# Native W_out products in column halves, from blocks that lie in natural order

## The chip, the cores and the metric

The kernel runs on one core of a Trainium2 chip. The metric is the device time of one execution in microseconds (us). A run of the kernel before comes with the median of three executions, and one more execution was taken by the hardware profiler; the trace below is of that one.

## What is computed

Attention with a sliding window of 128 and 4 sink positions, over 4 batches, 8 heads, 768 positions and head size 64, and behind it a two-layer perceptron with a leaky rectifier, all in fp32:

```python
def _moe_ref(x, w_in, w_out, alpha):           # x: 3072 x 512, the attention's output
    h = x @ w_in                               # 512 x 2048
    g = np.maximum(h, 0.0) + alpha * np.minimum(h, 0.0)
    return (g @ w_out).astype(np.float32)      # 2048 x 512
```

## The kernel before

The 3072 tokens are worked in 12 chunks (c) of 256. The 2048 inner columns are 16 blocks (f) of 128, each with its part of w_in and of w_out (W_out below). For every chunk and block, `gemm1` makes a 128 x 256 tile of h in PSUM (L991), ScalarE and VectorE make g of it (L995, L996), and `gemm2` adds g times the block of W_out to two banks of 128 tokens x 512 columns, one for each half j of the chunk.

Most products are made in three fp32r steps: g and the weights are split in a high and a low part, and high x high, high x low and low x high are added (L1048, L1049, L1046, the last for the low part of g). The weights arrive as 64-bit floats and are converted on the chip in the first 150 us (`convert_weights`). For the first WHOLE = 8 blocks and the first two chunks, W_out is not split yet: `convert_weights` leaves it whole in a tile `entire` (L440), g isn't split either, and one native fp32 product a half stands in for the three steps (`whole` in `gemm2`, L1037). In the trace such a product has two passes, so two records for each half. The two chunks and eight blocks make 16 such products of two halves, 64 records. Later, for chunk 2, `divide` splits these eight blocks (L476 the cast to the high part, on ScalarE or VectorE, L479 the subtraction).

A W_out block lies with its 256 even columns ahead of its 256 odd ones, since the host writes it so; whoever reads it goes across both halves (`"p (y x) -> p x y"`), so that neighbouring columns come from places 256 elements apart, and the result has the natural order.

The attention's values (`values`, L873; L971 for the last chunks) are native too, with 64 stationary columns each: two heads write to partitions 0 to 63 and 64 to 127 of one bank, in the two column halves of the array. Scores of the first two chunks (L670) are native products of two halves of 64 rows.

Nothing of the order on the engines is written out. Every operation is an `op` with an engine, an estimated cost, what it reads and writes, and `Plan.draw` simulates the engines with these costs and takes, for each engine, the ready operation of the lowest rank; `Plan.issue` writes the instructions in that order. For TensorE an operation may have a mode; where two operations that follow each other differ in it, the draw adds 0.16 us if one of the two is "col" and else 0.1. In the first 60 us, TensorE is given filling matmuls (L1221) where the draw sees it idle.

Of the kernel before, what the change touches and what calls it, by code (L numbers as in the profile page):

```python
# [9 lines left out]
F32 = mybir.dt.float32  # L10
# [7 lines left out]
ALU = mybir.AluOpType  # L18

P = 128  # L20
B, H, S, D = 4, 8, 768, 64
DM, DF = 512, 2048
# [6 lines left out]
NF = DF // P  # L29
# [28 lines left out]
WHOLE = 8  # L58
# [28 lines left out]
class Plan:  # L87
# [20 lines left out]
    def held(self, tile_):  # L108
        v = Value(None)
        v.at = tile_  # L110
        return v
# [197 lines left out]
def dve(n, fast=False):  # L309
    return 0.07 + (0.52e-3 if fast else 1.04e-3) * n  # L310


def cast(n, psum=False):
    return (0.045 if psum else 0.092) + 0.84e-3 * n
# [22 lines left out]
def woven(n):  # L337
    return 0.003 + 0.4167e-3 * n


def native(n):
    return 1.667e-3 * n
# [3 lines left out]
ISSUE = 0.45  # L346
SINKLAG = 0.0
R_TAIL, N_TAIL, T_TAIL = 0.2, 0.65, 0.36


def program(ctx, tc, qk, pairs, vp, vq, vs, w, par, out):
    nc = tc.nc
# [5 lines left out]
    op, val, held = plan.op, plan.value, plan.held  # L358
# [36 lines left out]
    raws, fins = {}, {}  # L395
# [7 lines left out]


    def home(f):
        return f + NF - WHOLE if f < WHOLE else f

    def load_weights(f, engine="ACT"):
        raw = raws[f] = held(None)

        def run():
            raw.at = const.tile([P, 2 * DM, 2], I32, tag=f"w{home(f)}", name="wraw")
            (nc.sync if engine == "SP" else nc.scalar).dma_start(
                raw.at.rearrange("p (i x) w -> p i (x w)", i=2), w[f].bitcast(I32).rearrange("i p x -> p i x"))
        return op(engine, ISSUE if engine == "SP" else 0.12, run, writes=[raw] + (lent.get(home(f), []) if f < WHOLE else [raws[f - NF + WHOLE]]), nbytes=8 * P * 2 * DM)

    def convert_weights(f):
        raw, fin, wa = raws[f], Block(None), val("wa")
# [51 lines left out]

    def divide(f):
        fin, entire = fins[f], entires[f]

        def high(engine):
            fin.at[1] = const.tile([P, 2, DM], F32R, tag=f"out{f - 1}", name="wout")
            (nc.scalar.copy if engine == "ACT" else nc.vector.tensor_copy)(fin.at[1][:, 0], entire.at)  # L476
        op("ACT", cast(DM), lambda: high("ACT"), reads=[entire], writes=[(fin, 2)] + ([entires[f - 1]] if f else []),
           other=("DVE", dve(DM, True), lambda: high("DVE")))
        op("DVE", dve(DM), lambda: nc.vector.tensor_tensor(  # L479
            fin.at[1][:, 1], entire.at, fin.at[1][:, 0].bitcast(F32), ALU.subtract), reads=[entire, (fin, 2)], writes=[(fin, 3)])  # L480

    stage, vtile, vst = {}, {}, {}

    lent = {}
# [64 lines left out]
    part, alt = param[:, :4], param[:, 4:].bitcast(F32)  # L549
# [313 lines left out]
    turned = {}  # L863
# [143 lines left out]
    def gemm2(c, f, dst):  # L1007
        gh, gl = gs.pop((c, f))
        fin = fins[f]
        begin, end = (WHOLE % NF, (WHOLE - 1) % NF) if c == 2 else (0, NF - 1)  # L1010
        if f == begin:
            acc[c] = [val("pa"), val("s")] if c == 1 else [val("o"), val("o")]
        o2 = acc[c]
        if c == NCHUNK - 1 and f >= NF - 2:
            latest.append((f, fin, gh, gl))
            for j in range(2 if f == NF - 1 else 0):
                for x, fin, gh, gl in latest:
                    def last(j=j, x=x, fin=fin, gh=gh, gl=gl):
                        js = slice(j * P, (j + 1) * P)
                        nc.tensor.matmul(o2[j].at, gh.at[:, js], fin.row(0), start=False, stop=False)  # L1020
                        nc.tensor.matmul(o2[j].at, gh.at[:, js], fin.row(1), start=False, stop=False)
                        nc.tensor.matmul(o2[j].at, gl.at[:, js], fin.row(0), start=False, stop=x == NF - 1)
                    op("PE", 3 * woven(DM), last, reads=[fin, gh, gl], writes=[o2[j]], tail=R_TAIL)
                ob = val("ob")
                for n, cols in enumerate((slice(0, DM // 2), slice(DM // 2, DM)) if j else (slice(0, DM),)):
                    op("ACT", cast(cols.stop - cols.start, True), lambda ob=ob, j=j, cols=cols: nc.scalar.copy(ob.at[:, cols], o2[j].at[:, cols]),  # L1026
                       reads=[o2[j]], writes=[(ob, n)])
                    by, cost, engine = ("ACT", 0.1, nc.scalar) if n == j else ("SP", ISSUE, nc.sync)
                    op(by, cost, lambda ob=ob, j=j, cols=cols, engine=engine: engine.dma_start(dst(j)[:, :, cols], ob.at[:, cols]),
                       reads=[(ob, n)], nbytes=4 * P * (cols.stop - cols.start))  # L1030
            return
        if c < 2 and f < WHOLE:
            entire = entires[f]

            def whole():
                for j in range(2):
                    nc.tensor.matmul(o2[j].at, gh.at[:, j * P:(j + 1) * P], entire.at.rearrange("p (y x) -> p x y", y=2),  # L1037
                                     start=f == begin, stop=False)
            op("PE", 2 * native(DM), whole, reads=[entire, gh], writes=o2, tail=N_TAIL)
            return  # L1040
        for lowpart in range(2):
            def some(lowpart=lowpart):
                for j in range(2):
                    js = slice(j * P, (j + 1) * P)
                    if lowpart:
                        nc.tensor.matmul(o2[j].at, gl.at[:, js], fin.row(0), start=False, stop=(f == end))  # L1046
                    else:
                        nc.tensor.matmul(o2[j].at, gh.at[:, js], fin.row(0), start=(f == begin), stop=False)  # L1048
                        nc.tensor.matmul(o2[j].at, gh.at[:, js], fin.row(1), start=False, stop=False)  # L1049
            op("PE", (2 if lowpart else 4) * woven(DM), some, reads=[fin, gl if lowpart else gh], writes=o2, tail=R_TAIL)  # L1050
        if f == end:
            for j in range(2):
                ob = val("ob")
                op("ACT", cast(DM, True), lambda ob=ob, j=j: nc.scalar.copy(ob.at, o2[j].at), reads=[o2[j]], writes=[ob],
           other=("DVE", dve(DM), lambda ob=ob, j=j: nc.vector.tensor_copy(ob.at, o2[j].at)) if 0 < c < 3 else None)
                op("SP", ISSUE, lambda ob=ob, j=j: nc.sync.dma_start(dst(j), ob.at), reads=[ob], nbytes=4 * P * DM)
            del acc[c]
# [109 lines left out]
    def dst(c):  # L1167
        return lambda j: out[c * QC:(c + 1) * QC].rearrange("(y j x) d -> j x y d", y=2, j=2)[j]
# [9 lines left out]
    n = 0  # L1178
# [35 lines left out]
    for a in pend:  # L1214
        gemm2(*a, dst(a[0]))
# [27 lines left out]
    gen = ctx.enter_context(tc.tile_pool(name="general", bufs=1))  # L1243
# [3 lines left out]
    wts = [fins[f].at for f in range(NF)]  # L1247
    with tc.If(bad != 0, label="general"):
        for f in range(NF):
            for i in range(2):  # L1250
                general_weights(nc, gen, w[f, i], wts[f][i])
        with tc.For_i(0, B, 1) as b:
            for cc in range(CPB):
                x = general(nc, gen, ptile, cc, b, qk5, vp5, nsink, window, ident)
                acc = [ptile("o", 2) for _ in range(2)]
                for f in range(NF):
                    general_moe(nc, gen, ptile, f, x, wts[f], alt, acc)
                for j in range(2):
                    ob = gen.tile([P, DM], F32, tag="ob", name="ob", bufs=3)
                    nc.scalar.copy(ob, acc[j])  # L1260
                    nc.gpsimd.dma_start(out5[b, cc, j], ob)
# [24 lines left out]
        nc.tensor.matmul(acc[j], gl[:, js], rows[0], start=False, stop=(f == NF - 1))  # L1286


def general_weights(nc, gen, src, dst):
    raw = gen.tile([P, DM, 2], I32, tag="wraw", name="wraw", bufs=2)  # L1290
    nc.gpsimd.dma_start(raw.rearrange("p x w -> p (x w)"), src.bitcast(I32))
    a = gen.tile([P, DM], I32, tag="wa", name="wa", bufs=2)
    low, high, af = raw[:, :, 0], raw[:, :, 1], a.bitcast(F32)
    nc.scalar.activation(af, high.bitcast(F32), AF.Abs)
    nc.vector.tensor_scalar(af, af, EXP_LOW, EXP_HIGH, op0=ALU.max, op1=ALU.min)
    nc.vector.tensor_scalar(a, a, 3, 0x3FFFFFFF, op0=ALU.logical_shift_left, op1=ALU.bitwise_and)
    nc.vector.scalar_tensor_tensor(a, high, -0x40000000, a, op0=ALU.bitwise_and, op1=ALU.bitwise_or)
    nc.scalar.activation(low, low.bitcast(U32), AF.Copy, scale=2.0 ** -29)
    nc.vector.tensor_tensor(a, a, low, ALU.add)
    nc.scalar.copy(dst[:, 0], af)  # L1300
    nc.vector.tensor_tensor(dst[:, 1], af, dst[:, 0].bitcast(F32), ALU.subtract)


def general(nc, gen, ptile, cc, b, qk5, vp5, nsink, window, ident):
# [118 lines left out]
```

## Time and profile before

| | us |
|---|---|
| median of three executions | 652.11 (651.16 to 652.94) |
| the profiled execution | 651.43 |
| its span, first to last instruction | 649.9 |
| busy in the span: TensorE | 640.4 (99%) |
| VectorE | 522.6 (80%) |
| ScalarE | 392.4 (60%) |

PE is TensorE's matmuls, PEld its loads of stationary operands, DVE VectorE, ACT ScalarE, POOL GpSimd. Matmuls are pipelined: a record lasts from its start to the arrival of its last result, and the next may start long before. So what an instruction costs is read from start to start, not from its duration, and a busy TensorE is not one without waits. Where a native matmul is followed by an fp32r one, the record of the latter starts early and lasts longer; the start of the one after it tells when the native one was through. An operand shape such as 128*64 128x512 is 128 rows by 64 stationary columns, then the moving operand.

### The profile page before, as it was taken

How to read it: one execution, taken by the hardware profiler on the slowest of the kernel's cores; microseconds unless marked ns; L12 is line 12 of the kernel's file. 1: busy time of each engine (PE TensorE's matmuls, PEld its weight loads, DVE VectorE, ACT ScalarE, POOL GpSimd, SP SyncE). 2: the span in 40 equal slices, each digit the busy share in tenths (PEclk: the TensorE clock that was granted, in tenths of full speed). 3: DMA queues.
4: the chain of work that ended last, by engine and by line, in shares of the span. 5: the costliest groups of instructions: out<-in, count | busy, mean ns of one | idle time of the engine just before them, and what ended most of it. 6: DMA issues, size and time to landing. Idle time of an engine off the chain costs nothing. (4 is left out here: it accounts for less than half of the span.)

```text
span 649.9 us, 13096 instructions
## 1 busy us (share of the span) xinstructions
PE 640.4 (99%) x4495; PEld 563.0 (87%) x4497; DVE 522.6 (80%) x1748; ACT 392.4 (60%) x1060; POOL 34.1 (5%) x115
## 2 busy tenths in 40 slices
PE   8999999989999999999999999999999999999997
PEld 3666667979998999999999999998999998998996
DVE  6998888997987987895996997895996997895332
ACT  6997677856646646645645754844754854752332
POOL 2120000000100000000100000000100000000000
PEclk9999999999999999999999999999999999999999
DMA  8776631333443444341633534432534424421001
GB/s 314 250 274 219 215 101 53 96 99 106 129 135 120 136 138 135 112 131 50 188 120 91 168 98 138 136 112 82 169 113 115 148 97 147 148 65 51 33 3 35
DMA packets 58825, 82.29 MB, mean 127 GB/s; under 512 B 9088, under 2 KB 35328, under 8 KB 58752
## 3 DMA queue, kind: packets, MB, share of 16 engines
q1 hardware_dynamic: 55200, 68.41, 33.3%
q10 hardware_dynamic: 3552, 12.98, 5.7%
q8 instruction: 37, 0.61, 0.4%
q14 instruction: 36, 0.29, 0.1%
HBM read 64.33 MB, written 17.04 MB: 125 GB/s over the span
## 5 line engine op out<-in xcount | busy, mean ns | idle before, releaser
L995 ACT ACTIVATE g<-bank,param 128x256 f32<-128x256 f32 x192 | 90.9, 473 | 94.4 <-PE bank L991 93.8
L991 PE MATMUL bank<-xh,win 128*128 128x256 f32 x768 | 140.5, 279 | 0.0
L991 PE MATMUL bank<-xh,w 128*128 128x256 f32 x768 | 139.1, 276 | 0.4 <-DVE g L996 0.4
L991 PEld LDWEIGHTS bank<-xh,w 128*128 128x128 f32 x768 | 120.9, 192 | 2.7 <-DVE g L996 1.0
L991 PEld LDWEIGHTS bank<-xh,win 128*128 128x128 f32 x768 | 120.8, 192 | 2.3 <-issue 1.6
L1001 ACT CAST gh<-g 128x256 fp32r<-128x256 f32 x176 | 70.6, 405 | 63.0 <-DVE g L996 62.4
L996 DVE TENSOR_TENSOR g<-bank,g 128x256 f32<-128x256 f32 x192 | 80.1, 420 | 33.8 <-ACT g L995 32.4
L991 PE MATMUL bank<-xl,win 128*128 128x256 f32 x384 | 105.7, 275 | 0.0
L991 PE MATMUL bank<-xl,w 128*128 128x256 f32 x384 | 105.6, 275 | 0.0
L700 ACT ACTIVATE pt<-pt,nm 128x260 f32<-128x260 f32 (+1 forms) x192 | 93.5, 489 | 16.5 <-DVE nm L694 16.2
L694 DVE CUSTOM_DVE_ANT_0 pt<-bank,masks 128x260 f32<-128x260 f32 (+1 forms) x192 | 71.2, 401 | 33.0 <-PE bank L680 29.3
L1002 DVE TENSOR_TENSOR gl<-g,gh 128x256 fp32r<-128x256 f32 x176 | 73.4, 421 | 17.6 <-ACT gh L1001 14.5
L991 PEld LDWEIGHTS bank<-xl,win 128*128 128x128 f32 x384 | 73.6, 192 | 2.3 <-issue 1.4
L991 PEld LDWEIGHTS bank<-xl,w 128*128 128x128 f32 x384 | 73.5, 192 | 1.2 <-issue 0.4
L1048 PE MATMUL bank<-w,gh 128*128 128x512 f32 x188 | 71.6, 381 | 0.0
L1049 PE MATMUL bank<-w,gh 128*128 128x512 f32 x188 | 71.2, 379 | 0.0
L641 ACT CAST kq<-stage 128x392 fp32r<-128x392 f32 (+1 forms) x80 | 39.1, 488 | 36.8 <-PE bank L680 28.2
L1048 PE MATMUL bank<-wout,gh 128*128 128x512 f32 x160 | 60.7, 379 | 0.0
L1049 PE MATMUL bank<-wout,gh 128*128 128x512 f32 x160 | 60.6, 379 | 0.0
L1046 PE MATMUL bank<-w,gl 128*128 128x512 f32 x188 | 56.4, 382 | 0.0
L1046 PE MATMUL bank<-wout,gl 128*128 128x512 f32 x160 | 47.7, 380 | 0.0
L745 POOL TENSOR_TENSOR sink<-pt,ri 128x8 f32<-128x8 f32 x80 | 20.2, 254 | 502.0 <-DVE ri L730 421.9
(150 smaller groups left out, 1106.3 us busy)
## 6 DMA issues: line engine op xcount, KB each, us to landing
stage<-qk SPq DMA_DIRECT2D x56, 324.0 KB, 2.9
wraw<-w ACTq DMA_DIRECT2D x12, 1024.0 KB, 5.2
swap<-comb SPq DMA_DIRECT2D x36, 256.0 KB, 2.0
comb<-swap SPq DMA_DIRECT2D x36, 256.0 KB, 3.0
stage<-qk SPq DMA_DIRECT2D x24, 260.0 KB, 2.7
out_dram<-ob SPq DMA_DIRECT2D x22, 256.0 KB, 2.7
v<-vq SPq DMA_DIRECT2D x24, 192.0 KB, 3.2
wraw<-w SPq DMA_DIRECT2D x4, 1024.0 KB, 9.2
```

The lines of the kernel that those rows point to most:

```text
L641: op("ACT", cast(KC - n), lambda: nc.scalar.copy(ks()[:, n:], k_raw()), reads=[st], writes=[(kq, "k")])
L694: o = op("DVE", dve(n), lambda: nc.vector.tensor_tensor_reduce(out=pt.at[:, u, w0], in0=s.at[:, w0], in1=masks[:, i, w0], scale=-0.125, sc ...
L700: op("ACT", exp(n), lambda: nc.scalar.activation(pt.at[:, u, w0], pt.at[:, u, w0], AF.Exp, bias=nm.at[:, h, u:u + 1], scale=-1.0, accum_ou ...
L745: op("POOL", 0.2, lambda: nc.gpsimd.tensor_tensor(sk.at[:, :, h], pt.at[:, :, P:P + NS], ri.at[:, :2].unsqueeze(2).broadcast_to([P, 2, NS] ...
L991: nc.tensor.matmul(h(), fin.win(part, ks), row, start=(kt == 0 and n == 0), stop=(kt == KT - 1 and n == 2))
L995: op("ACT", act(QC, True), lambda: nc.scalar.activation(g.at, h(), AF.Copy, scale=alt[:, f:f + 1]), reads=[bk, known("param")], writes=[g])
L996: op("DVE", dve(QC), lambda: nc.vector.tensor_tensor(g.at, h(), g.at, ALU.max), reads=[bk], writes=[g])
L1001: op("ACT", cast(QC), lambda: nc.scalar.copy(gh.at, g.at), reads=[g], writes=[gh])
L1002: op("DVE", dve(QC), lambda: nc.vector.tensor_tensor(gl.at, g.at, gh.at.bitcast(F32), ALU.subtract), reads=[g, gh], writes=[gl])
L1046: nc.tensor.matmul(o2[j].at, gl.at[:, js], fin.row(0), start=False, stop=(f == end))
L1048: nc.tensor.matmul(o2[j].at, gh.at[:, js], fin.row(0), start=(f == begin), stop=False)
L1049: nc.tensor.matmul(o2[j].at, gh.at[:, js], fin.row(1), start=False, stop=False)
```

## The change

The eight W_out blocks that are used whole lie in natural order, the host writes them so, and the native product reads its moving operand contiguously. Each product over 128 tokens becomes two over 64 tokens, which write to partitions 0 to 63 and 64 to 127 of the bank, so that they stand in the array's column halves; the operation has the mode "col" in the plan, at the same estimated cost. `divide`, which makes the split copies of the same blocks, writes them in the old order of even and odd columns, so it reads the whole block at every second element. The general branch, for inputs that the fast path doesn't cover, is adapted. `home` and the dependencies of the weights' loads are written in another way.

```diff
     def home(f):
-        return f + NF - WHOLE if f < WHOLE else f
+        return f + NF // 2 if f < WHOLE else f
...
-        return op(engine, ISSUE if engine == "SP" else 0.12, run, writes=[raw] + (lent.get(home(f), []) if f < WHOLE else [raws[f - NF + WHOLE]]), nbytes=8 * P * 2 * DM)
+        return op(engine, ISSUE if engine == "SP" else 0.12, run, writes=[raw] + ([raws[f - NF // 2]] if NF // 2 <= f < NF // 2 + WHOLE else lent.get(home(f), [])), nbytes=8 * P * 2 * DM)
...
     def divide(f):
         fin, entire = fins[f], entires[f]
+        turned_ = lambda: entire.at.rearrange("p (x y) -> p y x", y=2)
+        part = lambda n: fin.at[1][:, n].rearrange("p (y x) -> p y x", y=2)
...
-            (nc.scalar.copy if engine == "ACT" else nc.vector.tensor_copy)(fin.at[1][:, 0], entire.at)
+            (nc.scalar.copy if engine == "ACT" else nc.vector.tensor_copy)(part(0), turned_())
...
         op("DVE", dve(DM), lambda: nc.vector.tensor_tensor(
-            fin.at[1][:, 1], entire.at, fin.at[1][:, 0].bitcast(F32), ALU.subtract), reads=[entire, (fin, 2)], writes=[(fin, 3)])
+            part(1), turned_(), part(0).bitcast(F32), ALU.subtract), reads=[entire, (fin, 2)], writes=[(fin, 3)])
...
             def whole():
                 for j in range(2):
-                    nc.tensor.matmul(o2[j].at, gh.at[:, j * P:(j + 1) * P], entire.at.rearrange("p (y x) -> p x y", y=2),
-                                     start=f == begin, stop=False)
-            op("PE", 2 * native(DM), whole, reads=[entire, gh], writes=o2, tail=N_TAIL)
+                    for i in range(0, P, D):
+                        nc.tensor.matmul(o2[j].at[i:i + D], gh.at[:, j * P + i:j * P + i + D], entire.at, start=f == begin, stop=False)
+            op("PE", 2 * native(DM), whole, reads=[entire, gh], writes=o2, tail=N_TAIL, mode="col")
...
-    w[:, 1] = inputs['moe_w_out'].reshape(NF, P, DM // 2, 2).swapaxes(2, 3).reshape(NF, P, DM)
+    w[:, 1] = inputs['moe_w_out'].reshape(NF, P, DM)
+    w[WHOLE:, 1] = inputs['moe_w_out'].reshape(NF, P, DM // 2, 2)[WHOLE:].swapaxes(2, 3).reshape(NF - WHOLE, P, DM)
```

## Rows read from the trace of the kernel before

**Rows 1.** The page, part 1: busy us, share of the span, instructions.
```profile
PE 640.4 (99%) x4495; PEld 563.0 (87%) x4497; DVE 522.6 (80%) x1748; ACT 392.4 (60%) x1060; POOL 34.1 (5%) x115
```

**Rows 2.** Stages: stretch, length, busy PE, PEld, DVE, ACT, POOL, clock, DMA, GB/s.
```profile
30.00:60.00 30.00, 30.00 (x194) 19.69 (x192) 27.47 (x65) 26.44 (x64) 4.36 (x6) 1.00 0.73 248
60.00:110.00 50.00, 50.00 (x258) 33.93 (x256) 44.17 (x62) 37.50 (x58) 0.00 (x0) 1.00 0.38 135
110.00:135.00 25.00, 25.00 (x176) 23.23 (x175) 23.17 (x90) 19.60 (x57) 1.78 (x7) 1.00 0.31 96
135.00:147.00 12.00, 9.49 (x74) 7.50 (x73) 11.44 (x40) 4.99 (x13) 0.20 (x1) 1.00 0.23 68
147.00:649.90 502.90, 498.81 (x3635) 463.49 (x3634) 392.75 (x1405) 279.90 (x799) 22.06 (x75) 1.00 0.36 111
```

**Rows 3.** Timeline of PE (start, length, instruction, count): visits to L1037, first and last.
```profile
34.65 2.33 PE L1037 MATMUL bank<-wout,g 128*128 128x512 f32 x4
36.81 0.27 PE L719 MATMUL bank<-ident,pt 128*128 128x128 f32 x1
...
43.90 2.42 PE L1037 MATMUL bank<-wout,g 128*128 128x512 f32 x4
...
67.12 4.49 PE L1037 MATMUL bank<-wout,g 128*128 128x512 f32 x8
...
105.94 4.49 PE L1037 MATMUL bank<-wout,g 128*128 128x512 f32 x8
```

**Rows 4.** Timeline of PE: attention values in column halves, and what stands beside them.
```profile
16.09 1.52 PE L873 MATMUL bank<-comb,lent 128*64 128x256 f32 x16
17.55 0.33 PE L720 MATMUL bank<-ident,pt 128*128 128x128 f32 x1
...
54.12 1.96 PE L873 MATMUL bank<-comb,v 128*64 128x256 f32 x24
56.01 0.38 PE L991 MATMUL bank<-xh,win 128*128 128x256 f32 x1
...
140.87 0.40 PE L894 MATMUL bank<-sinkT,vs 128*128 128x256 f32 x2
141.21 0.44 PE L873 MATMUL bank<-wa,v 128*64 128x256 f32 x2
```

**Rows 5.** Waits from 50 to 95 us: total us, times, longest.
```profile
ACT g L995 <- PE bank L991: 9.4, 9, 2.4
```

**Rows 6.** Timeline of all engines at 100 and at 110 us.
```profile
100.22 0.42 DVE L476 CAST wout<-wout 128x512 fp32r<-128x512 f32 x1
...
110.38 0.28 PE L680 MATMUL bank<-kq 128*128 128x260 f32 x1
...
110.51 0.27 PE L991 MATMUL bank<-xh,w 128*128 128x256 f32 x1
...
110.70 0.43 DVE L694 CUSTOM_DVE_ANT_0 pt<-bank,masks 128x260 f32<-128x260 f32 x1 [1.14 <-PE bank L680]
```

**Rows 7.** Timeline of PE at 138 us: in brackets, idle before it and what ended it.
```profile
137.95 0.33 PE L815 MATMUL bank<-ident,comb 128*128 128x128 f32 x1 [1.43 <-DVE jk L741]
```

**Rows 8.** Groups of DVE by line and shape: count, busy us, mean ns, idle before.
```profile
L440 DVE SCALAR_TENSOR_TENSOR wout<-wraw,wa 128x512 int32<-128x512 int32 x8 | 5.5, 691 | 0.0
...
L479 DVE TENSOR_TENSOR wout<-wout 128x512 fp32r<-128x512 f32 x8 | 5.5, 685 | 0.1
L476 DVE CAST wout<-wout 128x512 fp32r<-128x512 f32 x2 | 0.8, 420 | 0.0
```

**Rows 9.** Groups of ACT by line and shape.
```profile
L423 ACT ACTIVATE wa<-wraw 128x1024 f32<-128x1024 f32 x16 | 20.1, 1254 | 0.1
...
L462 ACT CAST w<-wa 128x1024 fp32r<-128x1024 f32 x8 | 8.4, 1050 | 0.8 <-DVE wa L456 0.8
```

**Rows 10.** Timeline of PE at 120 us: fp32r products with a block of W_out.
```profile
119.86 0.38 PE L1048 MATMUL bank<-w,gh 128*128 128x512 f32 x1
120.08 0.38 PE L1049 MATMUL bank<-w,gh 128*128 128x512 f32 x1
```

More of the change, by code (lines that the diff above doesn't have):

```diff
@@ L1250, in program @@
             for i in range(2):
-                general_weights(nc, gen, w[f, i], wts[f][i])
+                general_weights(nc, gen, w[f, i], wts[f][i], f < WHOLE and i == 1)
         with tc.For_i(0, B, 1) as b:
@@ L1286, in general_moe, with general_weights @@
         nc.tensor.matmul(acc[j], gl[:, js], rows[0], start=False, stop=(f == NF - 1))
-def general_weights(nc, gen, src, dst):
+def general_weights(nc, gen, src, dst, turned):
     raw = gen.tile([P, DM, 2], I32, tag="wraw", name="wraw", bufs=2)
@@ L1299, in general_weights @@
     nc.vector.tensor_tensor(a, a, low, ALU.add)
-    nc.scalar.copy(dst[:, 0], af)
-    nc.vector.tensor_tensor(dst[:, 1], af, dst[:, 0].bitcast(F32), ALU.subtract)
+    high, low = [dst[:, n].rearrange("p (y x) -> p y x", y=2) for n in range(2)]
+    af = af.rearrange("p (x y) -> p y x" if turned else "p (y x) -> p y x", y=2)
+    nc.scalar.copy(high, af)
+    nc.vector.tensor_tensor(low, af, high.bitcast(F32), ALU.subtract)
 def general(nc, gen, ptile, cc, b, qk5, vp5, nsink, window, ident):
```

## The prediction

> **What bounds the kernel now.** I read the page first: TensorE is busy for 99% of the span [rows 1]. Busy says little for pipelined matmuls, so the table by stage comes next. Its granted clock is 1.00 (the 2.4 GHz level) in every stretch, so the clock is no part of the question. From 60 us on every stretch but one is filled: 50.00 of 50, 25.00 of 25, and 498.81 of 502.90 after 147 us; only 135 to 147 us has a hole (9.49 of 12), with VectorE at 11.44 of 12 [rows 2]. What is gained or lost before 147 us therefore reaches the end unchanged. The changed instructions all lie between 34.65 and 110.5 us: the timeline has six visits to L1037 of 4 records and five of 8, in all 64 records or 16 products (2 chunks x 8 blocks), each of two token halves in two passes [rows 3].
>
> **What a native pass costs now.** From 34.65 to the next start at 36.81 are 2.16 us for 4 passes; a visit of 8 lasts 4.49 against 2.33 for one of 4, again 2.16 more [rows 3]. Both give 0.54 us for a pass over 512 columns.
>
> **What a pass costs in column halves.** The trace has no product with W_out in that mode, but it has the attention values (L873): native, 64 stationary columns, two halves of one bank, the moving operand contiguous. One set of 16 records takes 1.46 us (16.09 to 17.55), one of 24 takes 1.89 (54.12 to 56.01) [rows 4]. The 8 records between them are four pairs of 128 columns, 512 columns for each half: 0.43 us. So the halves run side by side, and a pair of passes over 512 columns takes 0.43 where one full-width pass takes 0.54. A product keeps four such steps (2 groups of 128 tokens x 2 passes), so it falls from 2.16 to 1.72 us.
>
> **What the mode costs.** Three terms. Inside: 16 records are 1536 columns, 3 x 0.43 = 1.30 of the 1.46 measured, so 0.16 is fixed. Ahead: the second L894 starts at 140.99 (the pair's end, 141.27, less one's 0.28) and L873 at 141.21, 0.22 later [rows 4]; after a like instruction in the plain mode it is 0.13 (110.38 to 110.51) [rows 6]: 0.09. Behind: the first L991 after a visit lasts 0.38 [rows 4], a plain one 0.27 [rows 6]: 0.10. Together 0.35 us a visit.
>
> **Sum on TensorE.** A visit of one product: 2.16 - 1.72 - 0.35 = 0.09 us saved. A visit of two: 4.32 - 3.44 - 0.35 = 0.53. Six and five of them: 0.54 + 2.65 = 3.2. The visit at 43.90 comes behind a row-split product and lasts 2.42 instead of 2.33 already [rows 3]: some 0.1 to 0.2 of the mode's price is paid there today, so 3.3.
>
> **What of it counts.** The six single visits lie before 65 us. In 30 to 60 us VectorE is busy 27.47 of 30 [rows 2] and makes the blocks that TensorE works on; I count half of their 0.7. The five double ones, 2.65, lie from 67 us on, where VectorE has 5.8 us idle of 50 and ScalarE 12.5 [rows 2]. Both wait there for TensorE: ScalarE 9.4 us in nine waits of L995 for L991 between 50 and 95 us [rows 5], and VectorE at 110.70 for L680 directly, 1.14 us [rows 6]. With an earlier TensorE these waits move ahead; the 1.14 alone lets VectorE follow by that much, and the idle time ahead of it by the rest. After 110.70 VectorE is busy 23.17 of 25 to 135 us [rows 2], then TensorE waits 1.43 for L741 [rows 7]. If both enter that stage 3 us earlier, the hole moves as it is. So 0.35 + 2.65 = **3.0 us**.
>
> **The smaller parts.** The split copies of the eight blocks (`divide`) now read every second element. The subtractions (L479, 0.685) are like L440, which reads a stepped operand of as many elements in 0.691 [rows 8]: 0.01 each. For ScalarE's casts, a stepped read of 1024 (L423, another function) takes 1.254 against 1.050 for the contiguous cast L462 [rows 9]: at most 0.10 for 512, six times, beside the 12.5 us of idle. For VectorE's two casts the bounds are 0.42 (nothing changes) and 0.69 (the speed of L479 on as many elements) [rows 8]: 0 to 0.54 us in all. The first is at 100.22, the second behind it, ahead of the 1.14 us wait [rows 6], so I take nothing for them; without that cover they cost up to 0.5. A page of the Trainium skill (Advanced Engine Details and Errata, VectorE Performance Modes) asks for both operands in SBUF and even outer dimensions for the mode with two read ports, not for unit step; by it these casts stay at 0.42 and the sum stands. No run here shows it yet. How the split blocks lie and are read (`row`) is as before, and so are the loads: `home` and their dependencies give the same numbers at NF 16 and WHOLE 8. The general branch doesn't run.
>
> **The planner.** The order on all engines comes from `Plan.draw`, and the products now carry the mode "col", for which it charges TensorE 0.16 on entering and on leaving. So the written order can move, and with it the number of visits. I take 11, as now: nothing in the draw's choice looks at the mode. If all 16 products stood alone it would cost 5 x 0.35 = 1.75; if all stood in pairs, it would bring 1.05. A new order in the stage after 110 us may bring or cost about one wait of the size seen there, 1.4 [rows 7].
>
> **Forecast.** The profiled execution took 651.43 (span 649.9, and 1.5 around it), 0.68 below the median of three, 652.11. 651.43 - 3.0 = 648.4 in its terms, **649.1** in the median's.
>
> **Rivals.** (A) *The gain is lost at the hole.* VectorE, not TensorE, paces 110 to 140 us; if it can't start that stage earlier, TensorE only waits longer than 1.43 for L741. For it: 23.17 of 25 busy. Against: VectorE itself waits 1.14 for TensorE as the stage begins [rows 6]. Two thirds to all of the gain go: 651.1 to 652.1.
> (B) *Slower: the 0.11 us a pass are not the reading order's.* A W_out block lies with its even and odd columns in two halves and is read across them, and I put 0.54 against 0.43 down to that. But the same reading in fp32r takes 0.22 for 512 columns (119.86 to 120.08) [rows 10], 0.42 ns a column, while contiguous fp32r takes 0.13 for 260 [rows 6], 0.5: there it is the faster one. If a 512-column native pass costs 0.54 in any order, only the visits are left: 11 x 0.35 less 0.2, 3.6 us, 655.7. It decides from 0.48 a pass on (0.54 less 3.6 us over 64 steps). Against it, L873 shows one price a column over 16 and 24 records. On SBUF, the Trainium skill (SBUF — State Buffer, the note on cachelines) says that accesses which go to another 16-byte line each time pay for it. By that rule native passes lose by the old order and B falls away, but fp32r would lose too, and its rows say the opposite; so the rule takes little from B.
> (C) *The halves don't overlap on one and the same moving tile* (L873's read two): 128 passes of 0.43 are 55.0 us against 34.6; with the visits some 24 slower, 676.
> (D) *The new order is worse* by one or two waits of 1.4 after 110 us, or VectorE's casts add to it: 650.5 to 652.8.
>
> **How the numbers follow.** Forecast 0.55 (its own range 647.6 to 650.6, by the visits and the casts), A 0.20, D 0.13, B 0.10, C 0.02. About 0.3%, 2 us, is what a measurement of this kernel can tell from no change: faster means below 650.15. Of the forecast's 0.55 some 0.45 lies there, and 0.03 of A and D: faster 0.48. Slower is B, C and the end of D: 0.14. The rest, 0.38, is no difference. The range goes from 647.0 (pairs only, or a better order) to 652.8 (the end of D) and leaves B and C out.
>
> **What would show it.** The successor of L1037 as 128 records of 64 stationary columns, four steps of 0.43 a product and 0.35 for a visit; 0.54 a step is B, a product of 3.4 us is C. The first scores after 110 us near 107.5; if they are there and the hole at 136 is longer by as much, it is A. The casts of `divide` on VectorE at 0.42 or 0.69. More than 11 visits, or another hole after 110 us, is D. The forecast is wrong if any of these holds.

## The result and the profile after

The changed kernel takes 645.99 us (median of four, 645.96 to 646.20) against 651.77 for the kernel before (median of four, 651.16 to 652.94): a ratio of 0.991, 95% interval 0.9893 to 0.9927. It is 5.8 us faster where 3.0 were forecast, and 1.0 us below the range. The profiled execution took 646.20 with a span of 644.7, 5.2 below that of the kernel before.

The table by stage comes first, in the columns of [rows 2]. The stages are cut 3 to 4 us earlier, since the work now lies that much earlier.

```profile
30.00:60.00 30.00, 30.00 (x215) 18.84 (x215) 28.82 (x68) 26.79 (x65) 3.56 (x6) 1.00 0.66 239
60.00:106.90 46.90, 46.90 (x300) 31.53 (x298) 44.28 (x65) 37.18 (x58) 0.00 (x0) 1.00 0.43 151
106.90:131.00 24.10, 24.10 (x173) 22.89 (x172) 22.95 (x92) 20.13 (x58) 1.20 (x6) 1.00 0.33 100
131.00:143.00 12.00, 11.03 (x84) 9.29 (x83) 11.78 (x36) 5.02 (x14) 0.40 (x2) 1.00 0.24 68
143.00:644.70 501.70, 497.53 (x3630) 462.72 (x3628) 392.11 (x1405) 278.51 (x797) 22.00 (x75) 1.00 0.36 112
```

The fourth line is the surprise: in these 12 us TensorE is busy for 11.03, where [rows 2] had 9.49. Next, TensorE's timeline in the changed kernel: the first visit to the product (now L1040), the first double one, the last, and the start of the values of chunk 3 (L957, before: L955).

```profile
34.72 0.27 PE L722 MATMUL bank<-ident,pt 128*128 128x128 f32 x1
34.92 1.94 PE L1040 MATMUL bank<-wout,g 128*64 128x512 f32 x8
36.79 0.33 PE L721 MATMUL bank<-ident,pt 128*128 128x128 f32 x1
...
66.43 0.28 PE L993 MATMUL bank<-xh,win 128*128 128x256 f32 x1
66.63 3.65 PE L1040 MATMUL bank<-wout,g 128*64 128x512 f32 x16
70.22 0.38 PE L993 MATMUL bank<-xh,win 128*128 128x256 f32 x1
70.43 0.27 PE L993 MATMUL bank<-xl,win 128*128 128x256 f32 x1
...
103.35 3.65 PE L1040 MATMUL bank<-wout,g 128*64 128x512 f32 x16
106.94 0.39 PE L681 MATMUL bank<-kq 128*128 128x260 f32 x1
107.16 0.28 PE L682 MATMUL bank<-kq 128*128 128x260 f32 x1
...
191.05 0.40 PE L957 MATMUL bank<-sinkT,vs 128*128 128x256 f32 x2
```

And the same last mark in the kernel before:

```profile
196.32 0.40 PE L955 MATMUL bank<-sinkT,vs 128*128 128x256 f32 x2
```

A double visit lasts 3.59 us (66.63 to 70.22). Ahead of it 0.09 more is paid (0.20 from 66.43, where a plain step is 0.11), and 0.10 behind it (0.21 to 70.43). Together that is 3.78, where 3.44 + 0.35 = 3.79 was forecast. There are 11 visits, six of one product and five of two, as before.

With two marks the span falls into three parts. The first mark is the scores' second matmul behind the last visit (L680, now L682), the second is the start of L955 (now L957):

| | before | after | difference |
|---|---|---|---|
| to the first mark | 110.38 | 107.16 | -3.22 |
| from there to the second | 85.94 | 83.89 | -2.05 |
| from there to the end | 453.55 | 453.65 | +0.10 |

So up to the first mark the kernel gained what was summed for the instructions (3.2, or 3.3 with the visit at 43.90). Another 2.05 us came from the stage behind them. Of the waits that the timeline of TensorE marks between 107 and 150 us two are left:

```profile
134.33 0.44 PE L797 MATMUL bank<-ident,ts 128*128 128x128 f32 x2 [0.81 <-DVE ts L779]
134.93 0.44 PE L817 MATMUL bank<-ident,comb 128*128 128x128 f32 x2 [0.17 <-DVE wa L821]
```

The kernel before had four, the 1.43 us of [rows 7], 0.30 at 145.67, and these two:

```profile
138.49 0.60 PE L815 MATMUL bank<-ident,comb 128*128 128x128 f32 x2 [0.21 <-DVE jk L741]
...
140.10 0.38 PE L991 MATMUL bank<-xh,w 128*128 128x256 f32 x1 [0.44 <-DVE g L996]
```

The stretch of the first waits, about 136 to 140 us in the kernel before, is called the hole below.

The pieces of `divide`, in groups by line and shape as in [rows 8]: the casts on VectorE, then the subtractions, then the casts on ScalarE. The new plan gives one cast more to VectorE, three and five where it was two and six.

```profile
L478 DVE CAST wout<-wout 128x512 fp32r<-128x512 f32 x3 | 1.3, 425 | 0.0
...
L481 DVE TENSOR_TENSOR wout<-wout 128x512 fp32r<-128x512 f32 x8 | 5.8, 728 | 0.3 <-ACT wout L478 0.2
...
L478 ACT CAST wout<-wout 128x512 fp32r<-128x512 f32 x5 | 3.6, 720 | 0.4 <-DVE wout L481 0.4
```

VectorE's casts of every second element stay at 0.425 on the mean (before 0.420). ScalarE's take 0.72, 0.10 longer than before, and that 0.10 is the upper bound given. The subtractions take 0.04 more, not 0.01.

### The profile page after: what moved, and what is told of

It reads as the page before. It is cut to its first block, busy times and chain, and to the rows that moved or that the text cites. A ratio compares the mean times of both kernels' runs of the same rounds, so it can differ in the third digit from the quotient of the medians.

```text
span 644.7 us, 13231 instructions
## 1 busy us (share of the span) xinstructions
PE 637.2 (99%) x4559; PEld 560.8 (87%) x4561; DVE 523.3 (81%) x1749; ACT 391.5 (61%) x1059; POOL 33.1 (5%) x115
## 5 line engine op out<-in xcount | busy, mean ns | idle before, releaser
L993 PE MATMUL bank<-xh,w 128*128 128x256 f32 x768 | 138.7, 276 | 0.0
L993 PE MATMUL bank<-xh,win 128*128 128x256 f32 x768 | 138.5, 277 | 0.0
L993 PEld LDWEIGHTS bank<-xh,win 128*128 128x128 f32 x768 | 120.9, 192 | 4.6 <-ACT wraw L432 0.8
L993 PEld LDWEIGHTS bank<-xh,w 128*128 128x128 f32 x768 | 121.2, 192 | 2.5 <-DVE fm L710 0.8
L993 PE MATMUL bank<-xl,win 128*128 128x256 f32 x384 | 105.8, 276 | 0.0
L993 PE MATMUL bank<-xl,w 128*128 128x256 f32 x384 | 105.7, 275 | 0.0
L696 DVE CUSTOM_DVE_ANT_0 pt<-bank,masks 128x260 f32<-128x260 f32 (+1 forms) x192 | 71.2, 401 | 30.4 <-PE bank L682 26.6
L993 PEld LDWEIGHTS bank<-xl,w 128*128 128x128 f32 x384 | 73.6, 192 | 0.8
L993 PEld LDWEIGHTS bank<-xl,win 128*128 128x128 f32 x384 | 73.7, 192 | 0.6 <-DVE xl L943 0.2
L1050 PE MATMUL bank<-w,gh 128*128 128x512 f32 x188 | 71.6, 381 | 0.0
L1051 PE MATMUL bank<-w,gh 128*128 128x512 f32 x188 | 71.3, 379 | 0.0
L1050 PE MATMUL bank<-wout,gh 128*128 128x512 f32 x160 | 60.8, 380 | 0.0
L1051 PE MATMUL bank<-wout,gh 128*128 128x512 f32 x160 | 60.7, 379 | 0.0
```

The source lines that it names most:

```text
L696: o = op("DVE", dve(n), lambda: nc.vector.tensor_tensor_reduce(out=pt.at[:, u, w0], in0=s.at[:, w0], in1=masks[:, i, w0], scale=-0.125, sc ...
L993: nc.tensor.matmul(h(), fin.win(part, ks), row, start=(kt == 0 and n == 0), stop=(kt == KT - 1 and n == 2))
```

## The experiments

There are two theories of the 2.05 us. Theory 1: the mode "col" makes `Plan.draw` write another order for all engines, and that order has the shorter hole. Theory 2: the hole shrinks because TensorE comes earlier. The instructions and the plan can be changed apart. The kernels ran in three groups, each on a chip of its own and beside the kernel before: 652.56 us (15 executions) beside halves_old_order, fullwidth_new_order, natural_fullwidth and halves_old_layout; 652.4 (18) beside before_filled_hole, natural_old_order, before_true_cost and natural_other_cost; 652.06 (7) beside natural_third_order. Theories are numbered anew in each expectation.

**New instructions, old order.**

```diff
-            op("PE", 2 * native(DM), whole, reads=[entire, gh], writes=o2, tail=N_TAIL, mode="col")
+            op("PE", 2 * native(DM), whole, reads=[entire, gh], writes=o2, tail=N_TAIL)
```

> The changed kernel, but its products carry no mode in the plan, so that every engine gets the order of the kernel before. Theory 1 (the 2 us beyond the forecast come from the plan's new order, the instructions give the 3.3 us that were summed): about 648.5 us, 3.3 below the kernel before, and TensorE's hole between the last visit and 147 us as long as before (about 4 us). Theory 2 (the order is worth nothing; the hole shrinks because TensorE comes earlier to VectorE's work): about 646, the changed kernel's time.

Measured: 648.61 us (647.78 to 648.99), ratio 0.9926 (0.9912 to 0.994). TensorE's timeline, the two marks and the hole:

```profile
106.87 0.28 PE L682 MATMUL bank<-kq 128*128 128x260 f32 x1
...
134.47 0.33 PE L817 MATMUL bank<-ident,comb 128*128 128x128 f32 x1 [1.43 <-DVE jk L743]
135.00 0.60 PE L817 MATMUL bank<-ident,comb 128*128 128x128 f32 x2 [0.21 <-DVE jk L743]
...
136.62 0.38 PE L993 MATMUL bank<-xh,w 128*128 128x256 f32 x1 [0.44 <-DVE g L998]
...
193.91 0.29 PE L957 MATMUL bank<-sinkT,vs 128*128 128x256 f32 x1
```

The waits are those of before to the last digit, 1.43, 0.21 and 0.44, only 3.5 us earlier. So the hole does move as it is, as long as the order stays: theory 1. The first mark comes 3.51 us earlier than before (110.38 to 106.87), which is what the instructions give in this order. But the stage between the marks takes 87.04, 1.1 more than the 85.94 of before. Its table by stretch shows why:

```profile
132.00:137.00 5.00, 2.79 (x18) 1.80 (x17) 4.53 (x23) 2.60 (x9) 0.20 (x1) 1.00 0.00 0
...
137.50:138.00 0.50, 0.50 (x5) 0.28 (x4) 0.50 (x2) 0.00 (x0) 0.00 (x0) 0.50 0.00 0
138.00:140.70 2.70, 2.70 (x19) 1.94 (x20) 2.62 (x9) 0.66 (x1) 0.00 (x0) 0.50 0.39 97
...
141.50:147.00 5.50, 5.50 (x40) 4.90 (x41) 4.30 (x10) 2.87 (x6) 0.00 (x0) 1.00 0.26 82
```

After the hole (2.79 busy of 5 us) the granted clock is 0.50, the 1.2 GHz level, for some 3 us, and TensorE's work there runs at half speed: from one pair of passes over 256 columns to the next it takes 0.42 us, where it is 0.21 in the kernel before. The profiled execution of the kernel before has the same hole and kept its clock:

```profile
135.50:140.50 5.00, 2.79 (x18) 1.80 (x16) 4.53 (x23) 2.60 (x9) 0.20 (x1) 1.00 0.00 0
```

So this hole lets the clock fall in some executions and not in others.

**Old instructions, new order.** The same edit the other way round in the kernel before (`mode="col"` added, nothing else).

> The kernel before, but its products carry the mode col in the plan, so that every engine gets the order of the changed kernel; the instructions are the old ones (128 stationary columns, old layout). Theory 1 (the order alone brings about 2 us): 649.8 us, the passes at 0.54 us. Theory 2 (the order is worth nothing): 651.8 or more.

Measured: 649.32 us (649.24 to 649.62), ratio 0.9941 (0.9927 to 0.9954), clock 1.000 in all five.

```profile
110.51 0.28 PE L680 MATMUL bank<-kq 128*128 128x260 f32 x1
...
137.72 0.44 PE L795 MATMUL bank<-ident,ts 128*128 128x128 f32 x2 [0.81 <-DVE ts L777]
138.32 0.44 PE L815 MATMUL bank<-ident,comb 128*128 128x128 f32 x2 [0.16 <-DVE wa L819]
...
194.44 0.40 PE L955 MATMUL bank<-sinkT,vs 128*128 128x256 f32 x2
```

The first mark is where it was (110.51 against 110.38), and the stage takes 83.92, as in the changed kernel, with its two waits. One argument of the plan, with no instruction changed in kind, is worth 2 us of stage, and 3.2 in the medians, the rest of which is the clock's (below). The order is shown to be the second part of the gain. In this order the instructions give 3.35 us up to the first mark (110.51 to 107.16).

**The clock.** The medians of before, 651.77 to 652.56, lie above its profiled execution (651.43, clock 1.000). Among the 18 executions of the kernel before that ran in the second group, six had a mean clock of 1.000 and took 651.31 to 651.58; nine had 0.996 or 0.997 and took 651.89 to 653.01; three had 0.994 and took 653.62 to 653.99. To see whether the hole does this, the plan's filling matmuls were let go on: `WARM = 150.0` instead of 60 in the kernel before, which adds ten, all in the hole.

> The kernel before with the plan's filling matmuls allowed until 150 us instead of 60: ten more of them, all in the hole between 136 and 141 us; the order of all else is as before. If the hole lets TensorE's clock fall in most executions, and that makes the median 652.6 where an execution at clock 1.000 takes 651.4: clock 1.000 and about 651.4 us in all of them. If the hole itself is all: 652.6 or more, as fillings can only delay.

Measured: 651.44 us (651.23 to 651.64 in twelve executions), ratio 0.9987 (0.9978 to 0.9996), clock 0.999 or 1.000 in all. The start of the hole in TensorE's timeline:

```profile
136.19 1.47 PE L1221 MATMUL bank<-idle 128*128 128x512 bf16 x6
137.51 0.72 PE L815 MATMUL bank<-ident,comb 128*128 128x128 f32 x2
138.06 0.60 PE L1221 MATMUL bank<-idle 128*128 128x512 bf16 x2
```

With the hole filled by work of no use, the scatter is gone and the median is that of an execution at full clock; the stage between the marks is as long as before, 85.97. So the old order costs 2.05 us in this stage, and about 1 us in the median by the clock that falls after the hole in most executions. That it falls right there is seen in the profiles of halves_old_order and natural_old_order; no profile of the kernel before shows a fall. The changed kernel has neither loss, and its four executions differ by 0.24 us.

**What made the pass shorter, the order of reading or the halves?** The change does both. First natural order without the split, the plan as in the changed kernel:

```diff
-                    for i in range(0, P, D):
-                        nc.tensor.matmul(o2[j].at[i:i + D], gh.at[:, j * P + i:j * P + i + D], entire.at, start=f == begin, stop=False)
+                    nc.tensor.matmul(o2[j].at, gh.at[:, j * P:(j + 1) * P], entire.at, start=f == begin, stop=False)
```

> The changed kernel with blocks in natural order, but each product as one of 128 tokens over the full width of the array; the plan is the changed kernel's. If the reading order alone made a pass 0.54 us: passes of 0.43, no visits to pay (11 x 0.35), so 646.0 - 3.9 = 642.1 us. If a full-width native pass over 512 columns costs 0.54 whatever it reads: passes of 0.54, the time of the kernel before in the new order, 649.8 to 651.8.

Measured: **643.13 us** (642.95 to 643.42), ratio 0.9845 (0.983 to 0.9861): 2.9 below the changed kernel, the fastest of all, and 1.0 above the 642.1 expected.

```profile
34.73 1.88 PE L1039 MATMUL bank<-wout,g 128*128 128x512 f32 x4
36.45 0.27 PE L721 MATMUL bank<-ident,pt 128*128 128x128 f32 x1
...
104.19 0.28 PE L682 MATMUL bank<-kq 128*128 128x260 f32 x1
...
188.13 0.40 PE L957 MATMUL bank<-sinkT,vs 128*128 128x256 f32 x2
```

Four passes take 1.72 us (34.73 to 36.45), 0.43 each, over the full width and with no price for a visit. Then the split without the natural order, in the kernel before:

```diff
-                    nc.tensor.matmul(o2[j].at, gh.at[:, j * P:(j + 1) * P], entire.at.rearrange("p (y x) -> p x y", y=2),
-                                     start=f == begin, stop=False)
-            op("PE", 2 * native(DM), whole, reads=[entire, gh], writes=o2, tail=N_TAIL)
+                    for i in range(0, P, D):
+                        nc.tensor.matmul(o2[j].at[i:i + D], gh.at[:, j * P + i:j * P + i + D], entire.at.rearrange("p (y x) -> p x y", y=2),
+                                         start=f == begin, stop=False)
+            op("PE", 2 * native(DM), whole, reads=[entire, gh], writes=o2, tail=N_TAIL, mode="col")
```

> The kernel before with each product as two of 64 tokens in the column halves, but the blocks in the old layout, read across their two halves; the plan is the changed kernel's. If the reading order is what costs: steps of 0.54 and the visits on top, 646.0 + 64 x 0.11 = 653.0 us. If column halves hide it: steps of 0.43, 646.0.

Measured: 653.07 us (652.81 to 653.77), ratio 1.0006 (0.9996 to 1.0016), as expected to 0.1 us.

```profile
68.98 4.54 PE L1038 MATMUL bank<-wout,g 128*64 128x512 f32 x16
73.44 0.38 PE L991 MATMUL bank<-xh,win 128*128 128x256 f32 x1
```

A visit of two products lasts 4.46 us, 0.54 a step plus the mode. So the reading order is the whole of the 0.11 us a pass, and the column halves only add to the time: 645.99 with them, 643.13 without.

**Does an order's gain add to any instructions?** Natural order over the full width with the order of before (no mode):

> Blocks in natural order, each product over the full width, no mode in the plan: its estimate of 1.71 us for a product is now what a product takes (4 x 0.43), and the order on all engines is that of the kernel before. Theory 1 (this order has the longer hole near 136 us, whatever the instructions take): 2.0 us of hole and 0.5 to 1 us of lower clock more than with the changed kernel's order, 643.1 + 2.5 to 3 = 645.6 to 646.1 us. Theory 2 (the order was bad only since the plan took a product for 0.45 us shorter than it was): 643.1 or less.

Measured: 645.63 us (644.45 to 646.36; clock 0.996 or 0.997 in four executions, 1.000 in the one of 644.45). Its wait for L743 is again 1.43. The plan's estimate of a product, 1.71 us, is now right (4 x 0.43 = 1.72), so a wrong estimate is not what makes the hole of this order; theory 2 of this run falls. Up to the first mark these instructions gain 6.97 us in this order (110.38 to 103.41), all of the 64 x 0.11. Then a third order, from another estimate in the kernel before, `op("PE", 2.16, whole, ...)` in place of `2 * native(DM)`:

> The kernel before, but the plan takes 2.16 us for a product, as the trace shows, instead of 1.71; no mode, instructions as before; this gives a third order. Theory 2 (a truer cost gives a better order): 649.3 us or less, as with the changed kernel's order, and a clock of 1.0. Theory 1 (an order is a draw, good or bad by chance): anything between 649 and 653.

Measured: 649.12 us (649.05 to 649.42), ratio 0.9952 (0.9935 to 0.9968), clock 0.999 to 1.000; one wait of 0.73 in place of the hole. Both theories of this run allow that, so it decides nothing between them. And an estimate of `2 * native(DM) + 0.16` for the natural blocks over the full width:

> Blocks in natural order over the full width, no mode, the plan's estimate of a product 0.16 us longer (1.87); an order near that of the run with 2.16. Theory 1: the same gain or loss of order as that run has against the kernel before, that is 649.3 - 643.1 = 6.2 us below it within 0.5 us. Theory 2: worse than with the true estimate of 1.71.

Measured: 645.76 us (644.97 to 646.59), a miss for theory 1, which gave 643. The order is not near the third one: over a hundred of VectorE's 1748 operations stand elsewhere in it, and it has a wait of 1.61 for L743 again. Nor is it told apart from the 645.63 of natural_old_order, as theory 2 would have it. To part order from instructions the natural blocks were given exactly the third order (estimate 2.16):

> Blocks in natural order over the full width with the order of the run before_true_cost (the plan's estimate of a product 2.16 us, more than the 1.72 that it takes here). If an order's gain adds to the instructions' (theory 1): 6.2 us below before_true_cost, as natural_old_order stands to the kernel before with its clock falls, so 649.1 - 6.2 = 642.9 us, no hole over 1 us near 136, clock 1.0. If a truer estimate is what makes an order good (theory 2): this estimate is wrong by 0.44, so 645 to 646, with a hole as in natural_other_cost.

Measured: 645.33 us (645.17 to 645.49), ratio 0.9899 (0.9882 to 0.9915). A miss for both: the clock is 0.998 to 1.000 and the hole is gone, as theory 1 had it, but the time is 2.4 us more than it gave; the time is the one that theory 2 gave, but without the hole that was its reason. TensorE's timeline, one wait ahead of the last visit, the first mark and the wait that stands for the hole:

```profile
86.49 0.38 PE L993 MATMUL bank<-xh,w 128*128 128x256 f32 x1 [0.27 <-DVE g L998]
...
105.56 0.28 PE L682 MATMUL bank<-kq 128*128 128x260 f32 x1
...
134.04 0.44 PE L817 MATMUL bank<-ident,comb 128*128 128x128 f32 x2 [0.73 <-DVE wa L821]
```

The first mark is at 105.56, 4.92 ahead of before_true_cost (110.48), where the same instructions gain 6.32 in the changed kernel's order (110.51 to 104.19) and 6.97 in the old one. The loss lies ahead of the mark; TensorE's loads of stationary operands wait there for VectorE's g. From the waits of the loads between 30 us and the first mark, first this run, then natural_fullwidth:

```profile
PEld bank L993 <- DVE g L998: 3.2, 5, 1.0
```
```profile
PEld bank L993 <- DVE g L998: 1.9, 6, 0.5
```

In natural_old_order the same view lists no load of L993 that waits for g. VectorE is near its limit in all these kernels, but not nearer in this one. From 60 us to the first mark, natural_old_order and then natural_third_order:

```profile
60.00:103.40 43.40, 43.40 (x243) 32.24 (x242) 42.06 (x61) 37.04 (x57) 0.00 (x0) 1.00 0.41 146
```
```profile
60.00:105.50 45.50, 44.45 (x242) 32.01 (x241) 43.32 (x59) 37.47 (x58) 0.00 (x0) 1.00 0.44 163
```

VectorE is idle for 1.3 us in the first and for 2.2 in the second. So the loss is not a lack of time on VectorE but the sequence of its work: what the third order puts ahead of g holds up TensorE now that the products are shorter. That is read from these waits; no run moves a single operation. natural_fullwidth too gains only 2.97 us on the changed kernel up to the first mark (107.16 to 104.19), where 3.9 were expected.

All in one table, by marks (us; the first mark, the stage between the marks, the median):

| kernel | pass | order | first mark | stage | median |
|---|---|---|---|---|---|
| before | 0.54 | old | 110.38 | 85.94 | 651.8 to 652.6 |
| before_filled_hole | 0.54 | old | 110.30 | 85.97 | 651.44 |
| fullwidth_new_order | 0.54 | new | 110.51 | 83.92 | 649.32 |
| before_true_cost | 0.54 | third | 110.48 | 83.45 | 649.12 |
| halves_old_layout | 0.54, halves | new | 113.85 | 83.89 | 653.07 |
| halves_old_order | 0.43, halves | old | 106.87 | 87.04 | 648.61 |
| the changed kernel | 0.43, halves | new | 107.16 | 83.89 | 645.99 |
| natural_old_order | 0.43 | old | 103.41 | 87.02 | 645.63 |
| natural_other_cost | 0.43 | fourth | 103.39 | 86.44 | 645.76 |
| natural_third_order | 0.43 | third | 105.56 | 84.59 | 645.33 |
| natural_fullwidth | 0.43 | new | 104.19 | 83.94 | 643.13 |

The stage takes 83.9 in all four kernels with the new order, whatever their instructions, and 85.9 to 86.0 with the old one at full clock (87.0 in the two profiled executions whose clock fell). What comes after the second mark takes 453.5 to 453.9 in every one.

One thing shows only across the runs. Where W_out lies in the old layout, VectorE's casts of `divide` read contiguously and all eleven take 0.42 to 0.43 us, whatever TensorE does meanwhile. In natural order they read every second element, and their time goes with TensorE's work beside them: six of fourteen, beside native products for most of their length, take 0.42 to 0.43, and eight, beside fp32r products, 0.46 to 0.57. One of each, from the changed kernel (beside L1040) and from halves_old_order (beside L1050 and L1051):

```profile
93.65 0.42 DVE L478 CAST wout<-wout 128x512 fp32r<-128x512 f32 x1
```
```profile
99.07 0.57 DVE L478 CAST wout<-wout 128x512 fp32r<-128x512 f32 x1
```

The subtractions take at most 0.69 us in the old layout and up to 0.89 in natural order. No run was made to test what in TensorE's work does it.

## Why the prediction was wrong

The direction was right and the size was not; the time lies 1.0 us below the range. Of the 3.1 us between the forecast of 649.1 and the 645.99 measured, 2.05 are the plan's order, 0.68 the part between profiled execution and median that was carried along, and 0.2 the share of the visits that was taken off; the rest is scatter.

- *A pass in halves 0.43, a visit 0.35, 3.2 to 3.3 us on TensorE*: right. A double visit takes 3.78 against 3.79, there are 11 visits, and the first mark comes 3.22 us earlier. With the order held fixed the instructions give 3.35 (new order) to 3.51 (old order).
- *What of it counts, 3.0*: all of it did. There was no need to take off half of the single visits, 0.2 to 0.3 us.
- *The planner, taken as nothing*: this is the step that failed. The prediction says that the written order can move and that a new one "may bring or cost about one wait", 1.4; the value in its sum is zero, and the lower end of its range is 647.0. The order brought 2.05, shown with the instructions held fixed by fullwidth_new_order (85.94 to 83.92). It is not one wait but several: 1.43, 0.21, 0.44 and 0.30 are gone, 0.81 and 0.17 have come, 1.4 in all; the other 0.65 lies in the steps beside them and isn't placed. "The hole moves as it is" holds for the old order (halves_old_order shows it), but that order was not kept.
- *"The clock is no part of the question"*: failed as well. It was read from the one profiled execution, which was at 1.00. The 0.68 us between it and the median was carried along as a constant. In most executions of the kernel before the clock falls, after the hole as the filled hole tells; with the hole gone that part goes too. The two profiled executions differ by 5.2, which is 3.2 + 2.05 less the 0.1 behind the second mark. The medians differ by 5.8: 0.34 more because the median of before lies that much above its profiled execution, which is the clock's part (0.6 to 1.1 beside the other groups), and 0.21 because the changed kernel's profiled execution lies above its own median, which is scatter.
- *Rival A* (gain lost at the hole): no. The first scores behind the last visit reach VectorE's L696 at 107.92, not at 110.70 [rows 6], and the hole got no longer even in the old order. Yet the thought had substance: in natural_third_order waits for VectorE take most of the 1.4 us by which it gains less than natural_fullwidth.
- *Rival B* (the 0.11 us is not the reading order's): refuted by natural_fullwidth and halves_old_layout, a run for each side. The rule of the Trainium skill (SBUF — State Buffer, the note on cachelines) that an access to another 16-byte line each time pays for it was given too little weight; these native passes agree with it, 0.54 against 0.43. fp32r shows no such loss, 0.22 us for 512 columns read across two halves [rows 10], and there the measurement decides. But that fp32r is the faster one that way, as the prediction has it, is not shown: its contiguous row is an instruction of 260 columns, not 512, and instructions of one length weren't compared.
- *Rival C* (no overlap on one tile): refuted, steps of 0.43.
- *Rival D* (the new order is worse): the mechanism was there, its sign was the other. Its upper end of 652.8 is more than its terms give: 649.1 + 2 x 1.4 + 0.5 is 652.4.
- *The casts of `divide`*: VectorE's stay at 0.425 in the changed kernel. With that its trace agrees with the Trainium skill (Advanced Engine Details and Errata, VectorE Performance Modes), whose conditions for the mode with two read ports don't ask for unit step. In other runs the same casts took up to 0.57, so 0.42 doesn't hold beside any work of TensorE; all stay below the upper bound of 0.69. The subtractions cost 8 x 0.04 = 0.3 us more, where 0.01 each was taken; that doesn't show in the stage.

Open: which of the operations that VectorE does in another order closes the hole. The new order was only taken as a whole; a single exchange was not tried. One candidate: in the orders with a wait of 1.4 us or more (the old and the fourth) VectorE begins its last conversion of weights (L456, 1.2 to 1.4 us) behind the first mark, at 112.45 in the kernel before; in the new and the third it begins ahead of it, at 106.76 in the changed kernel. That is a coincidence in eleven traces, not a test.

## What to carry to other kernels

Where a planner writes the order, a change of one operation's cost or mode is two changes: make each alone (the plan's argument without the instructions, and the instructions without it), for here they gave 2 to 3 and 3.3 to 3.5 us. Look at the clock of all executions, not of the profiled one, before calling it settled, and look for the hole that it falls after. And split a compound edit before keeping it: natural order alone takes 643.13 us, 2.9 below the change that also paid for column halves.

## What the runs showed of the hardware

A native fp32 pass of 512 columns takes 0.43 us on a contiguous moving operand and 0.54 when neighbouring columns come alternately from two places 1 KB apart, over the full width as in column halves. Two column halves read one and the same tile at full rate, their steps 0.43 us each, but a visit to that mode costs 0.35 us: 0.09 ahead, 0.16 inside and 0.10 behind. After five microseconds in which TensorE was busy for 2.79, its granted clock stood at 0.50 (the 1.2 GHz level) for about 3 us of full work in halves_old_order, and stayed at 1.00 after the same hole in the profiled execution of the kernel before. Of 18 executions with this hole 12 had a mean clock below 0.998; with ten filling matmuls in it twelve of twelve had 0.999 to 1.000. A cast of 512 fp32 elements at every second element took VectorE 0.42 to 0.43 us beside native products on TensorE and 0.46 to 0.57 beside fp32r products; a contiguous one took 0.42 to 0.43 beside either.
